# Issuing the matmuls that read low parts last, within scores, value products, output and down pieces and gate and up products

## The chip, the core and the metric

The program runs on one core of one Trainium2 chip. The metric is the device time of one execution in microseconds; of the kernel before there are three runs. A core has TensorE (matrix products into PSUM; PE in the rows, its weight loads PEld), VectorE (DVE), ScalarE (ACT), GpSimd (POOL), SyncE (SP) and DMA queues. Each engine works through its own instruction queue in order and waits at semaphores for the others.

## What is computed

```
h = layernorm(x) * (1 + ca) + sa                  # x: 2048 x 576; sa..gb from silu(c) @ w_mod
q = h @ wq                                        # 32 heads of 128; 16 key/value heads
p = softmax(q @ k.T / sqrt(128))                  # the last 512 keys of the cache, all rows
x = x + ga * ((p @ v) @ wo)
h = layernorm(x) * (1 + cb) + sb
x = x + gb * ((relu(h @ W_gate) * (h @ W_up)) @ W_down)   # 576 -> 4608 -> 576
```

All of it is in float32.

## The kernel before

Every float32 operand is split in two parts of TensorE's reduced format: a high part (a rounded copy, made by ScalarE) and a low part (the value minus the high part, made by GpSimd, for `qlo` by VectorE). A product a x b becomes three matmuls into one PSUM accumulation: high x high, high x low and low x high. So each group of three needs two low parts, and these are the last of the operands to be ready.

The attention part runs over 128 units (L1651): a unit is one head and one block of 512 rows. In unit u TensorE issues, in the order that is written out by hand in that loop (the schedule is manual):

- the scores of unit u, `s_half` (L488), two halves of two key tiles each: `k` is stationary, `qhi` and `qlo` stream, 512 columns; VectorE reduces each half to its maximum (L501),
- the query projection of unit u + 1 (`qps`, L424, 14 matmuls), from which ScalarE makes `qhi` and VectorE `qlo` (L480),
- in units below 4 and from 108 on the small product `qm` (L530) by which the maxima are spread; it waits for VectorE's L522. In units below 4 the maxima (`mr`) are subtracted by matmuls (L587),
- an output piece (`wo_piece` of an earlier pair of heads: a 128 x 576 block in two column halves, each in its own PSUM bank, six matmuls of 288 columns in each half),
- the value product of unit u - 1, `pv_half` (L626), two halves of six matmuls of 512 columns: `hi` and `lo` are the exponentials' parts,
- a second output piece, and then the next unit.

`o_mul` (L641, VectorE) divides the finished value product by the sums. The output pieces take `ohi` and `olo` of a pair of heads as stationary and `woga` (or `againo`, read back by a DMA) as streaming operand, high and low in `w[0]` and `w[1]`. A piece's PSUM tile has one buffer; for most pieces a ScalarE copy (L693) puts the running sum into it first (the seed), after another copy (L669) has taken the piece before out of it.

The MLP part (from about 1590 us) runs over pairs of hidden tiles: `prod` (L1007) makes gate and up with seven matmuls into one bank each; `wop` holds three tiles of high parts (the third with some low rows in it) and two of low parts. GpSimd writes the low rows of the third tile (L794) and then the two low tiles (L795). `md_piece` uses the same `down_piece` (L651) as the attention output.

Of the kernel before, what the change touches and what calls it, by code (L numbers as in the profile page):

```python
# [25 lines left out]
H2 = D // 2  # L26
# [8 lines left out]
def kernel(  # L35
# [13 lines left out]
    nc = tc.nc  # L49
# [399 lines left out]
    NU = HKV * NQB * 2  # L449
# [6 lines left out]
    wqs, ks, vs, wos = {}, {}, {}, {}  # L456
    qhi, qlo, pthi, ptlo, ohi, olo = {}, {}, {}, {}, {}, {}
    pt_src = {}

    def unit(u):  # L460
        return UNITS[u]
# [21 lines left out]
    st_, t5, pt, hi_, lo_, bc, rb, ks_, pvps, done, o, bps = ({} for _ in range(12))  # L483
# [4 lines left out]
    def s_half(u, h):  # L488
        g, qb, hd = unit(u)
        k = ks[g]  # L490
        t = psS.tile([P, 2, 512], F32, tag="s", name=f"s{u}_{h}")
        st_[u, h] = t
        for j in range(2):
            kt = 2 * h + j
            ps = t[:, j, :]
            nc.tensor.matmul(ps, k[:, kt, :], qhi[u], start=True, stop=False)  # L496
            nc.tensor.matmul(ps, k[:, 4 + kt, :], qhi[u], start=False, stop=False)  # L497
            nc.tensor.matmul(ps, k[:, kt, :], qlo[u], start=False, stop=True)  # L498
        if h == 0:
            t5[u] = sp.tile([P, 12, 16], F32, tag="t5", name=f"t5_{u}", bufs=1)  # L500
        nc.vector.tensor_reduce(t5[u][:, 2 * h:2 * h + 2, :].rearrange("p k b -> p (k b)"),  # L501
                                t.rearrange("p k (b j) -> p (k b) j", j=32),
                                axis=AX.X, op=ALU.max, apply_transpose=True)
# [122 lines left out]
    def pv_half(u, h):  # L626
        g, qb, hd = unit(u)
        if h == 0:
            pvps[u] = psM.tile([P, 512], F32, tag="mm", name=f"pv{u}")
        ps, v, a, b = pvps[u], vs[g], hi_[u, h], lo_[u, h]  # L630
        for j in range(2):
            kt = 2 * h + j
            nc.tensor.matmul(ps, v[:, kt, :], a[:, j, :], start=(kt == 0), stop=False)  # L633
            nc.tensor.matmul(ps, v[:, 4 + kt, :], a[:, j, :], start=False, stop=False)  # L634
            nc.tensor.matmul(ps, v[:, kt, :], b[:, j, :], start=False, stop=(kt == 3))  # L635
        if h:
            done[u] = pvps.pop(u)

    def o_mul(u):
        o[u] = rb.pop(u)  # L640
# [10 lines left out]
    def down_piece(his, los, ws, i, qt, nm, pool=None, seed=None):  # L651
        sl = slice(qt * P, (qt + 1) * P)
        pool = pool or (psW, "w")
        ps = pool[0].tile([P, 2, 512], F32, tag=pool[1], name=nm) if seed is None else seed
        for half in range(2):
            cs = slice(half * H2, (half + 1) * H2)
            n = 0
            for hi, lo, w in zip(his, los, ws):
                for a, b in ((hi, 0), (hi, 1), (lo, 0)):
                    nc.tensor.matmul(ps[:, half, :H2], a[:, sl], w[b][:, cs],  # L660
                                     start=(n == 0 and seed is None), stop=(n == 5),
                                     skip_group_check=seed is not None)
                    n += 1
        av = acc[i].rearrange("p (h n) -> p h n", h=2)

        def add():
            adds[i] += 1
            if seed is not None:
                nc.scalar.copy(av, ps[:, :, :H2])  # L669
                return  # L670
            nc.vector.tensor_tensor(av, ps[:, :, :H2], av, op=ALU.add)  # L671

        return add
# [21 lines left out]
    def piece(n):  # L695
        add = wo_piece(*pieces[n][1:], seed=seeds.get(n))

        def end():
            add()
            put_seed(n + 1)  # L700

        (pend_act if n in seeds else pend).append(end)
        return n in seeds
# [303 lines left out]
    def prod(m, s, n, xx):  # L1007

        hs, w = hop[m // NFP, OPS[s][1]], wop[n]
        ps = pair[m, s][:, xx, :]  # L1010
        ops = []
        for t in range(2):
            ops += [(w[:, xx, t, :], hs[t]), (w[:, xx, 3 + t, :], hs[t]), (w[:, xx, t, :], hs[3 + t])]
        ops.append((w[:, xx, 2, :], hs[2]))
        for i, (a, c) in enumerate(ops):
            nc.tensor.matmul(ps, a, c, start=s not in heir(m) and i == 0 and s not in seeds_of(m), stop=i == len(ops) - 1,  # L1016
                             skip_group_check=True)
# [268 lines left out]
    def step(name, t, fn, *args):  # L1286
        sched.append((t + PLAN.get(name, 0), len(sched), fn, args))

    HOOK = (0, 4, 6, 9)
    e = 10 * NU  # L1290
# [298 lines left out]
    t = 546  # L1589
# [32 lines left out]
    step("M1", e + 1, next, mlp)  # L1622
    step("T.pv0", e + 2, pv_half, NU - 1, 0)
    step("T.pv1", e + 2, pv_half, NU - 1, 1)
    step("T.sum", e + 2, sum_pre, NU - 1)
    step("M2", e + 3, next, mlp)
    step("T.mix", e + 4, last_unit)
# [7 lines left out]
    def run(u, k):  # L1635
        t = 10 * u + k
        while sched and sched[-1][0] <= t:
            fn, args = sched.pop()[2:]
            fn(*args)
# [11 lines left out]
    for u in range(NU):  # L1651
# [51 lines left out]
        run(u, 6)  # L1703
        if 0 < u < NU - 1:
            pv_half(u - 1, 1)
        if 10 * u + 6 in at:
            piece(at[10 * u + 6])
        run(u, 7)
        if u:
            o_mul(u - 1)  # L1710
# [63 lines left out]
```

## Time and profile before

| | us |
|---|---|
| runs, median of three (lowest to highest) | 2861.74 (2859.02 to 2862.04) |
| profiled execution: span from the first to the last instruction | 2855.8 |
| TensorE busy in the span | 2815.0 |
| VectorE busy | 2246.8 |
| GpSimd busy | 2123.8 |
| ScalarE busy | 1476.7 |

The span is 5.9 us shorter than the median of the runs; what lies around it is not in the rows. TensorE's granted clock was at the higher of its two levels nearly throughout (mean 0.998). A matmul's record ends by a model, later than the next matmul starts, so "busy" and "idle" of TensorE are read together with the starts.

### The profile page before, as it was taken

How to read it: one execution, taken by the hardware profiler on the slowest of the kernel's cores; microseconds unless marked ns; L12 is line 12 of the kernel's file. 1: busy time of each engine (PE TensorE's matmuls, PEld its weight loads, DVE VectorE, ACT ScalarE, POOL GpSimd, SP SyncE). 2: the span in 40 equal slices, each digit the busy share in tenths (PEclk: the TensorE clock that was granted, in tenths of full speed). 3: DMA queues.
4: the chain of work that ended last, by engine and by line, in shares of the span. 5: the costliest groups of instructions: out<-in, count | busy, mean ns of one | idle time of the engine just before them, and what ended most of it. 6: DMA issues, size and time to landing. Idle time of an engine off the chain costs nothing.

```text
span 2855.8 us, 41174 instructions
## 1 busy us (share of the span) xinstructions
PE 2815.0 (99%) x15006; PEld 2449.5 (86%) x15006; DVE 2246.8 (79%) x3384; ACT 1476.7 (52%) x2105; POOL 2123.8 (74%) x1564
## 2 busy tenths in 40 slices
PE   6999999999999999999999999999999999999999
PEld 5788888888888888888888888888888888888888
DVE  7899999999889998888889756676677466666666
ACT  5766666666766666666656444444444122222221
POOL 5688888888899989877778766788777356656653
PEclk9999999999999999999999999999999999999999
DMA  4012132222232213312243456666667844444442
GB/s 163 24 45 79 65 106 85 83 82 100 95 104 94 92 62 131 105 70 80 68 155 139 150 213 229 231 240 231 234 234 261 338 165 154 155 155 159 159 154 106
DMA packets 164506, 399.57 MB, mean 140 GB/s; under 512 B 15056, under 2 KB 62160, under 8 KB 164304
## 3 DMA queue, kind: packets, MB, share of 16 engines
q1 hardware_dynamic: 132912, 284.69, 29.9%
q10 hardware_dynamic: 31392, 112.26, 10.0%
q8 instruction: 118, 1.93, 0.3%
q14 instruction: 84, 0.69, 0.1%
HBM read 271.16 MB, written 154.57 MB: 149 GB/s over the span
## 4 chain that ended last, share of the span: by engine, by line
PE 83%; DVE 6%; POOL 5%; issue 2%; ACT 2%; DMA 2%; SPq 0%; ACTq 0%; DVEq 0%; POOLq 0%
PE gu L1016 26%; PE wo L660 12%; PE qps L424 11%; PE md L660 8%; PE st_P L1118 6%; PE s L498 3%; PE s L497 3%; PE s L496 3%; PE pv L635 3%; PE pv L634 3%; PE pv L633 3%; POOL lo L600 2%; DVE t L501 1%; DVE p L591 1%; POOL wop L795 1%
## 5 line engine op out<-in xcount | busy, mean ns | idle before, releaser
L600 POOL TENSOR_TENSOR lo<-p,hi 128x1024 fp32r<-128x1024 f32 x256 | 610.6, 2406 | 1.1 <-ACT hi L577 1.1
L609 POOL TENSOR_TENSOR ks<-ks,p 128x512 f32<-128x512 f32 x256 | 351.7, 1374 | 238.7 <-DVE ks L606 135.5
L501 DVE TRANSPOSE_TENSOR_REDUCE t<-s 128x32 f32<-128x1024 f32 x256 | 313.8, 1239 | 85.9 <-PE s L498 76.6
L1016 PE MATMUL gu<-hop_B,wop 128*128 128x512 f32 x1512 | 375.0, 391 | 0.2 <-POOL wop L795 0.2
L1016 PEld LDWEIGHTS gu<-hop_B,wop 128*128 128x128 f32 x1512 | 274.9, 188 | 51.1 <-POOL wop L795 0.9
L1016 PE MATMUL gu<-hop_T,wop 128*128 128x512 f32 x1260 | 316.1, 391 | 0.0
L424 PE MATMUL qps<-hTa,wA 128*128 128x512 f32 x1288 | 312.9, 394 | 3.1 <-DVE hTa L372 1.6
L660 PE MATMUL wo<-woga,ohi 128*128 128x288 f32 x1472 | 298.8, 295 | 2.0 <-POOL woga L183 1.4
L591 DVE TENSOR_TENSOR p<-s,mb 128x1024 f32<-128x1024 f32 x246 | 290.3, 1219 | 4.2
L424 PEld LDWEIGHTS qps<-hTa,wA 128*128 128x128 f32 x1288 | 244.5, 190 | 56.6 <-DVE hTa L372 3.2
L476 ACT ACTIVATE qhi<-qps 128x512 fp32r<-128x512 f32 x128 | 76.4, 597 | 366.9 <-PE qps L424 358.4
L660 PEld LDWEIGHTS wo<-woga,ohi 128*128 128x128 f32 x1472 | 245.9, 188 | 18.8 <-POOL woga L183 3.4
L1016 PEld LDWEIGHTS gu<-hop_T,wop 128*128 128x128 f32 x1260 | 227.8, 188 | 39.0
L577 ACT CAST hi<-p 128x1024 fp32r<-128x1024 f32 x256 | 259.5, 1042 | 1.5
L660 PE MATMUL md<-wogb,hhi 128*128 128x288 f32 x1272 | 256.9, 295 | 0.4 <-DVE acc L671 0.4
L593 ACT ACTIVATE p<-p 128x1024 f32<-128x1024 f32 x246 | 249.5, 1051 | 13.7 <-DVE p L591 13.4
L671 DVE TENSOR_TENSOR acc<-md,acc 128x576 f32<-128x576 f32 x159 | 119.9, 755 | 160.4 <-PE md L660 159.8
L660 PEld LDWEIGHTS md<-wogb,hhi 128*128 128x128 f32 x1272 | 210.9, 188 | 12.6 <-DVE acc L671 1.4
L1127 DVE TENSOR_TENSOR acc<-st_P,acc 128x576 f32<-128x576 f32 x160 | 121.1, 757 | 127.9 <-PE st_P L1118 127.9
L660 PE MATMUL wo<-woga,olo 128*128 128x288 f32 x736 | 217.8, 296 | 1.3 <-POOL olo L649 1.2
L660 PE MATMUL md<-wogb,hlo 128*128 128x288 f32 x636 | 187.5, 295 | 0.0
L649 POOL TENSOR_TENSOR olo<-rb,ohi 128x512 fp32r<-128x512 f32 x128 | 167.4, 1308 | 15.2 <-ACT ohi L645 15.0
(283 smaller groups left out, 7095.3 us busy)
## 6 DMA issues: line engine op xcount, KB each, us to landing
wop<-wk_P SPq DMA_DIRECT2D x133, 640.0 KB
wk_P<-wop ACTq DMA_DIRECT2D x119, 640.0 KB
wr<-wlay SPq DMA_DIRECT2D x68, 384.0 KB
rogb<-wd SPq DMA_DIRECT2D x68, 288.0 KB
againq<-akq SPq DMA_DIRECT2D x18, 640.0 KB
rwA<-wq SPq DMA_DIRECT2D x32, 320.0 KB
wlay<-wg SPq DMA_DIRECT2D x36, 256.0 KB
roga<-wo SPq DMA_DIRECT2D x32, 288.0 KB
```

The costliest lines, as they stand in the source:

```text
L424: return [lambda i=i, a=a, b=b: nc.tensor.matmul(ps, a, b, start=(i == 0), stop=(i == n - 1)) for i, (a, b) in enumerate(ops)]
L501: nc.vector.tensor_reduce(t5[u][:, 2 * h:2 * h + 2, :].rearrange("p k b -> p (k b)"), t.rearrange("p k (b j) -> p (k b) j", j=32), axis=AX ...
L577: nc.scalar.copy(hi_[u, h], pt[u, h])
L591: nc.vector.tensor_tensor(p, t, bc[u][:, None, :].to_broadcast([P, 2, 512]), op=ALU.subtract)
L593: nc.scalar.activation(p, p, AF.Exp, bias=0.0, scale=1.0)
L600: nc.gpsimd.tensor_sub(lo_[u, h], pt[u, h], hi_[u, h].bitcast(F32))
L609: nc.gpsimd.tensor_tensor(ks_[u], ks_[u], p[:, j, :], op=ALU.add)
L649: nc.gpsimd.tensor_sub(olo[u], o.pop(u), ohi[u].bitcast(F32))
L660: nc.tensor.matmul(ps[:, half, :H2], a[:, sl], w[b][:, cs], start=(n == 0 and seed is None), stop=(n == 5), skip_group_check=seed is not None)
L1016: nc.tensor.matmul(ps, a, c, start=s not in heir(m) and i == 0 and s not in seeds_of(m), stop=i == len(ops) - 1, skip_group_check=True)
L1118: nc.tensor.matmul(ps[:, j, :H2], x[:, sl], w[:, y, :], start=n == 0 and not second, stop=n == 2, skip_group_check=True)
L1127: nc.vector.tensor_tensor(t, ps[:, :, :H2], t, op=ALU.add)
```

## The change

In four places the matmuls that read a low part come after those that read only high parts, as far as the group goes; the operands and the sums are the same.

- `s_half`: the two key tiles' high products first, then the two that read `qlo`.
- `pv_half` leaves the `lo` products out; a new `pv_lows` issues all four. It stands directly behind the second `pv_half` in odd units; in even units the second output piece stands in between.
- `down_piece` (output and down pieces): in each column half four matmuls (both high x high, the first low x high, the first high x low), then in each half the other two.
- `prod`: the products with `wop`'s low tiles come last, with the third tile ahead of them.

```
-            ps = t[:, j, :]
-            nc.tensor.matmul(ps, k[:, kt, :], qhi[u], start=True, stop=False)
-            nc.tensor.matmul(ps, k[:, 4 + kt, :], qhi[u], start=False, stop=False)
-            nc.tensor.matmul(ps, k[:, kt, :], qlo[u], start=False, stop=True)
+            nc.tensor.matmul(t[:, j, :], k[:, kt, :], qhi[u], start=True, stop=False)
+            nc.tensor.matmul(t[:, j, :], k[:, 4 + kt, :], qhi[u], start=False, stop=False)
+        for j in range(2):
+            nc.tensor.matmul(t[:, j, :], k[:, 2 * h + j, :], qlo[u], start=False, stop=True)
...
-            nc.tensor.matmul(ps, v[:, kt, :], b[:, j, :], start=False, stop=(kt == 3))
-        if h:
-            done[u] = pvps.pop(u)
+    def pv_lows(u):
+        g, qb, hd = unit(u)
+        ps, v = pvps.pop(u), vs[g]
+        for kt in range(4):
+            nc.tensor.matmul(ps, v[:, kt, :], lo_[u, kt // 2][:, kt % 2, :], start=False, stop=kt == 3)
+        done[u] = ps
...
-            for hi, lo, w in zip(his, los, ws):
-                for a, b in ((hi, 0), (hi, 1), (lo, 0)):
+        ops = [(his[0], ws[0][0]), (his[1], ws[1][0]), (los[0], ws[0][0]), (his[0], ws[0][1]),
+               (his[1], ws[1][1]), (los[1], ws[1][0])]
+        for part in ((0, 1, 2, 3), (4, 5)):
+            for half in range(2):
...
-            ops += [(w[:, xx, t, :], hs[t]), (w[:, xx, 3 + t, :], hs[t]), (w[:, xx, t, :], hs[3 + t])]
-        ops.append((w[:, xx, 2, :], hs[2]))
+            ops += [(w[:, xx, t, :], hs[t]), (w[:, xx, t, :], hs[3 + t])]
+        ops += [(w[:, xx, 2, :], hs[2]), (w[:, xx, 3, :], hs[0]), (w[:, xx, 4, :], hs[1])]
...
             pv_half(u - 1, 1)
+            if u % 2:
+                pv_lows(u - 1)
         if 10 * u + 6 in at:
             piece(at[10 * u + 6])
+        if 0 < u < NU - 1 and u % 2 == 0:
+            pv_lows(u - 1)
```

TensorE, first half of the scores of unit 45, before and then after (names carry the unit; `kv5_0` is the key tile set):

```order
L496 MATMUL s45_0_6300<-qhi45_6222,kv5_0_5419 128x512
L497 MATMUL s45_0_6300<-qhi45_6222,kv5_0_5419 128x512
L498 MATMUL s45_0_6300<-qlo45_6260,kv5_0_5419 128x512
L496 MATMUL s45_0_6300<-qhi45_6222,kv5_0_5419 128x512
L497 MATMUL s45_0_6300<-qhi45_6222,kv5_0_5419 128x512
L498 MATMUL s45_0_6300<-qlo45_6260,kv5_0_5419 128x512
```

```order
L495 MATMUL s45_0_6300<-qhi45_6222,kv5_0_5419 128x512
L496 MATMUL s45_0_6300<-qhi45_6222,kv5_0_5419 128x512
L495 MATMUL s45_0_6300<-qhi45_6222,kv5_0_5419 128x512
L496 MATMUL s45_0_6300<-qhi45_6222,kv5_0_5419 128x512
L498 MATMUL s45_0_6300<-qlo45_6258,kv5_0_5419 128x512 x2
```

The two matmuls that read `qlo45` stood third and sixth; now they are fifth and sixth. Both key tiles' sums are open at once, each in its bank.

TensorE, even unit 66: the second half of the value product of unit 65 and the start of the piece behind it, before; then the end of that piece and what follows it, after:

```order
L633 MATMUL pv65_9015<-hi65_1_8933,kv8_1_8685 128x512
L634 MATMUL pv65_9015<-hi65_1_8933,kv8_1_8685 128x512
L635 MATMUL pv65_9015<-lo65_1_8940,kv8_1_8685 128x512
L633 MATMUL pv65_9015<-hi65_1_8933,kv8_1_8685 128x512
L634 MATMUL pv65_9015<-hi65_1_8933,kv8_1_8685 128x512
L635 MATMUL pv65_9015<-lo65_1_8940,kv8_1_8685 128x512
L660 MATMUL wo63_2_9023<-woga_14_7792,ohi62_8689 128x288 x2
L660 MATMUL wo63_2_9023<-woga_14_7792,olo62_8691 128x288
L660 MATMUL wo63_2_9023<-woga_15_8113,ohi63_8876 128x288 x2
```

```order
L666 MATMUL wo63_2_9021<-woga_14_7792,ohi62_8689 128x288 x2
L666 MATMUL wo63_2_9021<-woga_15_8113,ohi63_8876 128x288
L666 MATMUL wo63_2_9021<-woga_14_7792,olo62_8691 128x288
L666 MATMUL wo63_2_9021<-woga_14_7792,ohi62_8689 128x288
L666 MATMUL wo63_2_9021<-woga_15_8113,ohi63_8876 128x288
L666 MATMUL wo63_2_9021<-woga_15_8113,olo63_8878 128x288
L666 MATMUL wo63_2_9021<-woga_15_8113,ohi63_8876 128x288
L666 MATMUL wo63_2_9021<-woga_15_8113,olo63_8878 128x288
L640 MATMUL pv65_9015<-lo65_0_8938,kv8_1_8685 128x512 x2
L640 MATMUL pv65_9015<-lo65_1_8940,kv8_1_8685 128x512 x2
```

The four reads of `lo65` are behind the piece now, directly ahead of the scores of unit 67. In the piece the reads of `olo63` (the pair's second head) are the last of each half.

TensorE, the gate product `gu45` of one hidden tile, before and after (`hop0_B11_0` to `_2` are high parts, `_3` and `_4` low; an x2 reads a high and then a low weight tile):

```order
L1016 MATMUL gu45_19733<-hop0_B11_0_16355,wop63_19657 128x512 x2
L1016 MATMUL gu45_19733<-hop0_B11_3_16358,wop63_19657 128x512
L1016 MATMUL gu45_19733<-hop0_B11_1_16356,wop63_19657 128x512 x2
L1016 MATMUL gu45_19733<-hop0_B11_4_16359,wop63_19657 128x512
L1016 MATMUL gu45_19733<-hop0_B11_2_16357,wop63_19657 128x512
```

```order
L1021 MATMUL gu45_19733<-hop0_B11_0_16355,wop63_19657 128x512
L1021 MATMUL gu45_19733<-hop0_B11_3_16358,wop63_19657 128x512
L1021 MATMUL gu45_19733<-hop0_B11_1_16356,wop63_19657 128x512
L1021 MATMUL gu45_19733<-hop0_B11_4_16359,wop63_19657 128x512
L1021 MATMUL gu45_19733<-hop0_B11_2_16357,wop63_19657 128x512
L1021 MATMUL gu45_19733<-hop0_B11_0_16355,wop63_19657 128x512
L1021 MATMUL gu45_19733<-hop0_B11_1_16356,wop63_19657 128x512
```

The products with the two low weight tiles were second and fifth (the second of each x2) and are now the last two. On VectorE, ScalarE and GpSimd the instructions stand in the same order before and after.

## Rows read from the trace of the kernel before

**Rows 1.** The page: busy time of each engine, share, instructions
```profile
PE 2815.0 (99%) x15006; PEld 2449.5 (86%) x15006; DVE 2246.8 (79%) x3384; ACT 1476.7 (52%) x2105; POOL 2123.8 (74%) x1564
```

**Rows 2.** Table by stage, 600 to 1000 us: length, busy time by engine, clock, DMA
```profile
600.00:1000.00 400.00, 396.95 (x2070) 343.51 (x2069) 362.80 (x616) 275.12 (x382) 357.50 (x229) 1.00 0.29 94
```

**Rows 3.** TensorE's waits: who waited for whom, us in total, times, longest us
```profile
PE wo L660 <- POOL woga L183: 1.4, 3, 0.7
PE wo L660 <- POOL olo L649: 1.2, 5, 0.5
PE pv L635 <- POOL lo L600: 1.1, 2, 0.6
PE s L498 <- DVE qlo L480: 0.9, 2, 0.7
PE gu L1016 <- POOL wop L795: 0.6, 3, 0.2
PE wo L660 <- DMA againo<-ako: 0.3, 1, 0.3
```

**Rows 4.** The weight loads' waits, same columns
```profile
PEld pv L635 <- POOL lo L600: 3.9, 9, 1.0
PEld wo L660 <- POOL woga L183: 3.4, 8, 0.9
PEld s L498 <- DVE qlo L480: 3.4, 5, 1.1
PEld wo L660 <- POOL olo L649: 2.7, 6, 0.7
PEld gu L1016 <- POOL wop L795: 2.6, 7, 0.6
```

**Rows 5.** Timeline of TensorE around two waits: start us, length us, instruction, [idle before]
```profile
479.01 0.30 PE L660 MATMUL wo<-woga,ohi 128*128 128x288 f32 x1
479.67 0.40 PE L660 MATMUL wo<-woga,ohi 128*128 128x288 f32 x1 [0.36 <-POOL woga L183]
481.08 0.40 PE L497 MATMUL s<-qhi,kv 128*128 128x512 f32 x1
481.62 0.50 PE L498 MATMUL s<-qlo,kv 128*128 128x512 f32 x1
481.95 0.40 PE L496 MATMUL s<-qhi,kv 128*128 128x512 f32 x1
```

**Rows 6.** Timeline of unit 80 (even): seed copy and the second piece
```profile
1017.82 0.64 ACT L669 COPY acc<-wo 128x576 f32<-128x576 f32 x1 [1.04 <-PE wo L660]
1018.49 0.64 ACT L693 COPY wo<-acc 128x576 f32<-128x576 f32 x1
1020.31 0.42 PE L660 MATMUL wo<-woga,ohi 128*128 128x288 f32 x2
1020.97 0.29 PE L660 MATMUL wo<-woga,olo 128*128 128x288 f32 x1
1021.10 0.43 PE L660 MATMUL wo<-woga,ohi 128*128 128x288 f32 x2
```

**Rows 7.** Timeline of units 124 and 125: `o_mul`, scores, L522, `qm`
```profile
1554.91 0.68 DVE L641 TENSOR_TENSOR rb<-pv,rb 128x512 f32<-128x512 f32 x1
1555.62 0.39 PE L496 MATMUL s<-qhi,againk 128*128 128x512 f32 x1
1560.66 0.70 DVE L522 TRANSPOSE_TENSOR_REDUCE t<-ks 128x16 f32<-128x512 f32 x1
1561.55 0.34 PE L530 MATMUL qm<-t,quad 128*128 128x80 f32 x2
```

**Rows 8.** Timeline of unit 1: `mr`, the fifth value matmul, the matmuls that need `mr`
```profile
57.62 0.62 ACT L569 CAST mr<-mb 128x512 fp32r<-128x512 f32 x1 [7.67 <-DVE mb L566]
57.98 0.39 PE L634 MATMUL pv<-hi,kv 128*128 128x512 f32 x1
58.44 1.09 PE L587 MATMUL s<-mr,minus 128*128 128x512 f32 x4
```

More of the change, by code (lines that the diff above doesn't have):

```diff
@@ L629, in pv_half @@
             pvps[u] = psM.tile([P, 512], F32, tag="mm", name=f"pv{u}")
-        ps, v, a, b = pvps[u], vs[g], hi_[u, h], lo_[u, h]
+        ps, v, a = pvps[u], vs[g], hi_[u, h]
         for j in range(2):
@@ L654, in down_piece @@
         ps = pool[0].tile([P, 2, 512], F32, tag=pool[1], name=nm) if seed is None else seed
-        for half in range(2):
-            cs = slice(half * H2, (half + 1) * H2)
-            n = 0
-            for hi, lo, w in zip(his, los, ws):
-                for a, b in ((hi, 0), (hi, 1), (lo, 0)):
-                    nc.tensor.matmul(ps[:, half, :H2], a[:, sl], w[b][:, cs],
+        ops = [(his[0], ws[0][0]), (his[1], ws[1][0]), (los[0], ws[0][0]), (his[0], ws[0][1]),
+               (his[1], ws[1][1]), (los[1], ws[1][0])]
+        for part in ((0, 1, 2, 3), (4, 5)):
+            for half in range(2):
+                cs = slice(half * H2, (half + 1) * H2)
+                for n in part:
+                    a, w = ops[n]
+                    nc.tensor.matmul(ps[:, half, :H2], a[:, sl], w[:, cs],
                                      start=(n == 0 and seed is None), stop=(n == 5),
                                      skip_group_check=seed is not None)
-                    n += 1
         av = acc[i].rearrange("p (h n) -> p h n", h=2)
@@ L1624 @@
     step("T.pv1", e + 2, pv_half, NU - 1, 1)
+    step("T.pv2", e + 2, pv_lows, NU - 1)
     step("T.sum", e + 2, sum_pre, NU - 1)
```

## Prediction

> **What bounds the kernel now.** I read four views. The page's busy line comes first: TensorE is busy 2815.0 of 2855.8 us [rows 1], so no other engine can give back more than the gaps in its stream. The table by stage says how far the others are behind it: between 600 and 1000 us TensorE works 396.95 of 400 us, VectorE 362.80 and GpSimd 357.50 [rows 2]. TensorE is the bound, and the two that make the operands run close enough to be late now and then. The third view, TensorE's waits [rows 3], lists where: on `lo` (GpSimd) in the value product, on `olo` and the low half of `woga` (GpSimd) in the output pieces, on `qlo` (VectorE) in the scores, on the low rows of `wop` (GpSimd) in gate and up. Together 1.1 + 1.2 + 1.4 + 0.9 + 0.6 = 5.2 us in 15 waits. The weight loads' own list has the same five names, 3.9 + 2.7 + 3.4 + 3.4 + 2.6 = 16.0 us in 35 waits [rows 4]. Those two sums are the bounds of what this change can touch.
>
> The fourth view shows what one wait costs. Output matmuls start 0.13 us apart; at 479.01 the next started only at 479.67, 0.53 late, though the row calls 0.36 of it idle [rows 5]. A score matmul's record is 0.39 to 0.40 long while the next one starts 0.23 later [rows 5, 8]: the record's last 0.16 us hides as much of every wait. And the start after a wait is late once more: 481.62 to 481.95 is 0.33 instead of 0.23 [rows 5]. So a wait with idle time costs its idle time + 0.16 + 0.10.
>
> The Trainium skill's page "TensorE: Matmul & The Clock Gate" (section "Step-by-step: what each phase is for") says that weight loads are pulled ahead of matmuls in flight, so the next weights load while this matmul runs. By that rule the second delay would not exist and 15 × 0.10 = 1.5 us would fall out of the sum; the start at 481.95 speaks against it here, since the load behind a waiting one came late as well.
>
> **What the change removes.** No instruction comes or goes; the same matmuls stand in another order, and VectorE, ScalarE and GpSimd keep theirs. Sum of the waits: 5.2 + 15 × 0.16 + 15 × 0.10 = 9.1 us. In the 20 other waits only the load was late: each costs between nothing and 0.26 us, I take half, 2.6. That is 11.7 us, between 5.2 and 16.0.
>
> How much of each goes depends on how far its reader moves back.
> - Value product: in an even unit the second half's low read goes from ninth place to behind a whole output piece (two matmuls of 0.23 and twelve of 0.13 more): 2 us, against waits of at most 0.6 + 0.16 [rows 3]. Gone. In odd units it moves two matmuls, 0.45 us.
> - Scores: the first read of `qlo` goes from third to fifth, 0.45 us. The longest wait cost 0.7 + 0.16 = 0.86; 0.41 stays, and its 0.10.
> - Output pieces: the low half of the second weight goes from fifth to ninth, the second `olo` from sixth to tenth, 4 × 0.13 = 0.53 us. Of the longest waits 0.86 - 0.53 = 0.33 and 0.66 - 0.53 = 0.13 stay, with 0.10 each.
> - Gate and up: the low rows go from second to sixth, 0.9 us, against at most 0.2 + 0.16. Gone.
>
> What stays: 0.51 + 0.43 + 0.23 = 1.2 us. Gain: 11.7 - 1.2 = 10.5 us.
>
> **What it costs.** Four things are moved nearer to what they wait for.
> - In even units the value product now ends behind the piece, right ahead of the next scores, and `o_mul` (L641) on VectorE waits for it. In front of the scores that began at 1555.62 it started at 1554.91 [rows 7]; the last low matmul would start 0.23 before the scores and be done 0.39 after its start, at 1555.78: 0.87 later. Queued behind it are the L886 combinations, the two score reductions and L522. Where VectorE sat idle before the next reduction that is free. From 1520 to 1590 it did not: L522 ended at 1561.36 and the `qm` matmul that needs it ran at 1561.55 [rows 7], 0.19 of slack. So `qm` waits 0.87 - 0.19 = 0.68 us, three times (behind units 122, 124 and 126, where the same work stands on VectorE): 2.0 us. Bounds: 0 and 3 × 0.87 = 2.6.
> - In units 1 to 3 the first half of the value product covers the making of `mr`: six matmuls up to 58.44, `mr` done at 58.24 [rows 8]. With four, TensorE is there at 57.98 and waits 0.26 + 0.10; three times, 1.1 us (nothing, if a later wait of that stage shrinks by it).
> - In a piece the second pair's high halves are read two matmuls earlier; the one wait on `againo` [rows 3] grows by 0.26 us.
> - In even units the second piece starts four matmuls, 0.91 us, earlier. Its PSUM tile is seeded by a ScalarE copy that ended at 1019.13, the piece began at 1020.31 [rows 6]: of 1.18 us 0.27 stay. I take nothing.
>
> The 119 more waits in gate and up (the third weight tile now asks for itself) cost nothing where they are met when reached; the seven late loads on `wop` [rows 4] are what the trace has of the other kind.
>
> Costs 2.0 + 1.1 + 0.3 = 3.4. Net 10.5 - 3.4 = 7.1 us. The profiled span would become 2848.7; the median of the runs stands 5.9 above the span and I keep that: **2861.7 - 7.1 = 2854.6 us**. A measurement of this kernel can tell about 0.2%, 5.7 us, from no change, so this lies just beyond it, at 2856.0.
>
> **The rivals.**
> 1. *The waits come back.* A TensorE that is earlier meets the next late operand: VectorE had 37 and GpSimd 42 us of slack in 400 [rows 2]. For it: a wait also gives the late engine time to catch up. Against it: the reads that follow move back by 0.45 us or more too. If half the gain returns, 5.2 - 3.4 = 1.8 us: 2859.9.
> 2. *The waits cost what the loads show.* 16.0 - 1.2 - 3.4 = 11.4 us: 2850.3. For it: every late load delays what is behind it. Against: a load is early by up to one matmul, and part of its wait is free.
> 3. *Slower: the seed copy.* The margin left in even units is 0.27 us [rows 6], 63 units, of which 233 in 256 pieces have such a copy, so about 57. Each 0.1 us by which the copy comes later than that costs 57 × 0.1 = 5.7 us; it eats the whole gain from 0.27 + 7.1 / 57 = 0.40 us on. At 0.5 it is 57 × 0.23 = 13 us: 2867.7. For it: the copy stands on ScalarE between exponentials of 1 us. Against: ScalarE had been idle 1.04 us when the piece ended [rows 6], so nothing stands in front.
> 4. *The order itself costs.* Pieces and score halves now change their PSUM bank three times instead of once: two more in each of 416 pieces and 256 halves, 1344. At 1020.97 to 1021.10 such a change takes the usual 0.13 [rows 6]; the row is good to 5 ns, so up to 1344 × 0.005 = 6.7 us either way. On the bad side: 2861.3.
>
> That the build undoes the change is excluded by the order of instructions.
>
> **How the numbers follow.** The forecast 0.55, rival 1 0.20, rival 2 0.14, rival 3 0.05, rival 4 0.06. Faster by over 0.2% (below 2856.0): rival 2 whole and most of the forecast, 0.14 + 0.48 = 0.62. Within: the rest of the forecast, rivals 1 and 4, 0.07 + 0.20 + 0.06 = 0.33. Slower: 0.05. The range goes from a little under rival 2, since its costs may be nothing, to between rivals 1 and 4: 2848.5 to 2861.0, which leaves out rival 3 and the tails.
>
> **What would show it.** Right: the five names nearly vanish from TensorE's waits, one each on `qlo` and `woga` left under 0.5 us; the span is 6 to 8 us shorter; new entries are `qm` on VectorE's L522 near 1530, 1555 and 1580 of about 0.7 and `s` on `mr` three times. Rival 1: the names stay with fewer microseconds each. Rival 3: the seed copy L693 (L698 there) heads the releasers of output pieces. Rival 4: no waits, but matmuls of unchanged number in more busy time. The forecast is wrong if the five names go and the span does not follow.

## The result and the profile after

| | before | after |
|---|---|---|
| runs on one chip, median of eight each (lowest to highest), us | 2860.22 (2857.31 to 2862.04) | 2866.68 (2862.70 to 2867.57) |
| profiled execution: span, us | 2855.8 | 2860.6 |

The ratio is 1.0022, with a 95% interval of 1.0013 to 1.0031: the change made the kernel slower by about 6 us where 7 less were forecast. The predicted range ended at 2861.0. One execution of e2 below, 3086.97 us at a granted clock of 0.851, is in no median and no ratio here.

The page of the changed kernel, busy time and the chain that ended last:

```profile
PE 2817.1 (98%) x15006; PEld 2451.6 (86%) x15006; DVE 2249.3 (79%) x3384; ACT 1477.6 (52%) x2105; POOL 2123.9 (74%) x1564
...
PE 90%; DVE 5%; DMA 1%; POOL 1%; ACT 1%; issue 1%; SPq 0%; DVEq 0%; POOLq 0%; ACTq 0%
```

The chain stays on TensorE for 90% of the span. Its 15006 matmuls are busy 2.1 us longer than before [rows 1], and the span grew by 4.8; so some of the loss lies within busy time and some in new waits. TensorE's waits in the changed kernel (us in total, times, longest):

```profile
PE qm L530 <- DVE t L522: 5.7, 6, 1.3
PE s L587 <- ACT mr L569: 3.2, 3, 2.1
...
PE md L666 <- DVE acc L676: 2.4, 1, 2.4
...
PE s L498 <- DVE qlo L480: 0.8, 2, 0.6
PE wo L666 <- POOL woga L183: 0.7, 2, 0.3
PE gu L1021 <- DMA wop<-wk_P: 0.6, 1, 0.6
...
PE wo L666 <- POOL olo L653: 0.4, 1, 0.4
PE wo L666 <- DMA againo<-ako: 0.4, 1, 0.4
```

Beside [rows 3], what the change aimed at did happen: `lo` is gone from the list, `woga` and `olo` fell from 2.6 us in eight waits to 1.1 in three. The stage that was busiest with such waits shows it too: between 600 and 1000 us TensorE is busy 398.82 us, where [rows 2] had 396.95.

```profile
600.00:1000.00 400.00, 398.82 (x2081) 345.62 (x2080) 366.57 (x617) 276.41 (x383) 360.26 (x231) 1.00 0.29 94
```

New at the head of the list is `qm` behind VectorE, 5.7 us, and a down piece (`md`) with one wait of 2.4.

Where the 5 us came from is best read from landmarks: the start of the first score matmul of a unit, of the first gate and up product, and of the last matmul. The table has the difference to the same landmark in the trace of before, split into four stretches (us; minus is earlier). It lists all kernels of the experiments below; each row is one profiled execution.

| kernel | up to unit 12 | units 12 to 116 | unit 116 to the MLP | MLP | all |
|---|---|---|---|---|---|
| changed | +0.9 | -4.6 | **+7.0** | +1.8 | +5.1 |
| changed, again (e11) | +0.7 | -4.6 | +6.8 | +3.2 | +6.0 |
| no piece in between (e1) | -0.8 | -4.7 | -0.1 | -0.6 | -6.2 |
| piece in between to unit 107 (e4) | +2.8 | -4.6 | -0.1 | +0.4 | -1.5 |
| low products in mid piece (e5) | +1.3 | -3.6 | +0.9 | -0.6 | -2.1 |
| changed, piece as before (e2) | +0.2 | -0.9 | +7.5 | +6.5 | +13.4 |
| before, only the piece changed (e3) | -1.3 | -2.8 | 0.0 | +6.9 | +2.7 |
| e1, bank after bank (e6) | +3.0 | -0.8 | -0.1 | +1.4 | +3.6 |
| e1, four-six-two (e7) | +2.3 | -8.4 | -0.4 | -0.7 | -7.1 |
| e1, early lows inside (e8) | +1.2 | -4.5 | -0.1 | -1.1 | -4.4 |
| e1, alternating (e9) | +0.4 | -7.3 | -0.3 | +4.5 | -2.7 |
| changed, four-six-two (e10) | +1.1 | -7.7 | +6.8 | +1.4 | +1.6 |
| before, four-six-two (e12) | 0.0 | -6.2 | -0.4 | +2.0 | -4.5 |

The second and third columns repeat: the changed kernel's two profiles agree within 0.3 us there. The first and the last don't; what lies in them is told in the last section.

### The profile page after: what moved, and what is told of

The parts are those of the page before. It is cut to its first block, busy times and chain, and to the rows that moved or that the text cites. A ratio compares the mean times of both kernels' runs of the same rounds, so it can differ in the third digit from the quotient of the medians.

```text
span 2860.6 us, 41113 instructions
## 1 busy us (share of the span) xinstructions
PE 2817.1 (98%) x15006; PEld 2451.6 (86%) x15006; DVE 2249.3 (79%) x3384; ACT 1477.6 (52%) x2105; POOL 2123.9 (74%) x1564
## 4 chain that ended last, share of the span: by engine, by line
PE 90%; DVE 5%; DMA 1%; POOL 1%; ACT 1%; issue 1%; SPq 0%; DVEq 0%; POOLq 0%; ACTq 0%
PE gu L1021 28%; PE wo L666 13%; PE qps L424 12%; PE md L666 9%; PE st_P L1123 6%; PE pv L633 4%; PE s L495 4%; PE pv L634 4%; PE pv L640 4%; PE s L498 4%; PE s L496 4%; DVE t L501 1%; POOL lo L600 0%; DVE p L591 0%; DVE roga L223 0%
## 5 line engine op out<-in xcount | busy, mean ns | idle before, releaser
L609 POOL TENSOR_TENSOR ks<-ks,p 128x512 f32<-128x512 f32 x256 | 351.2, 1372 | 239.0 <-DVE ks L606 129.1
L676 DVE TENSOR_TENSOR acc<-md,acc 128x576 f32<-128x576 f32 x159 | 119.9, 755 | 164.5 <-PE md L666 164.0
L666 PE MATMUL wo<-woga,olo 128*128 128x288 f32 x736 | 211.2, 295 | 0.6 <-POOL olo L653 0.4
```

What stands on the lines that cost most here:

```text
L609: nc.gpsimd.tensor_tensor(ks_[u], ks_[u], p[:, j, :], op=ALU.add)
L666: nc.tensor.matmul(ps[:, half, :H2], a[:, sl], w[:, cs], start=(n == 0 and seed is None), stop=(n == 5), skip_group_check=seed is not None)
```

## The loss at the end of the attention part

Theory A: the output piece that now stands ahead of the low value products makes `o_mul` late, and by it VectorE's row of work up to `qm`. The prediction had this step, at 2.0 us. Here is unit 125 in the changed kernel: the first score matmul, `o_mul` (L645), the two combinations (L891), GpSimd's L609, L522 and `qm` (start, length, idle before):

```profile
1554.76 0.40 PE L495 MATMUL s<-qhi,againk 128*128 128x512 f32 x1
1554.96 0.69 DVE L645 TENSOR_TENSOR rb<-pv,rb 128x512 f32<-128x512 f32 x1 [0.83 <-PE pv L640]
1555.08 3.00 POOL L609 TENSOR_TENSOR ks<-ks,p 128x512 f32<-128x512 f32 x2 [1.75 <-ACT p L593]
1555.57 1.37 DVE L891 TENSOR_TENSOR lfb<-lfb,lfb 128x512 f32<-128x512 f32 x1
1556.85 1.77 DVE L891 TENSOR_TENSOR h<-h,h 128x512 f32<-128x512 f32 x1
...
1561.39 0.70 DVE L522 TRANSPOSE_TENSOR_REDUCE t<-ks 128x16 f32<-128x512 f32 x1
...
1562.15 0.45 PE L530 MATMUL qm<-t,quad 128*128 128x80 f32 x2 [1.32 <-DVE t L522]
```

and the two rows of the kernel before that answer to L609 and the first L891 (there L886):

```profile
1555.51 0.68 DVE L886 TENSOR_TENSOR lfb<-lfb,lfb 128x512 f32<-128x512 f32 x1
...
1555.95 3.10 POOL L609 TENSOR_TENSOR ks<-ks,p 128x512 f32<-128x512 f32 x2 [1.74 <-ACT p L593]
```

`o_mul` started 0.71 us ahead of the scores [rows 7] and now starts 0.20 behind them: 0.91 later, where 0.87 was predicted. But the combination behind it takes 1.37 us instead of 0.68. Before, it started 0.44 ahead of GpSimd's L609; now L609 is already under way. So the delay is 0.91 + 0.69 = 1.60, less the slack of 0.19 it is 1.41; `qm` runs 7.39 us after the first score matmul instead of 5.93 [rows 7], 1.46 later. Of the slack 0.13 could be used: L522 ends at 1562.09 here and `qm` starts 0.06 behind it.

**e1, no piece in between.**

```
             pv_half(u - 1, 1)
-            if u % 2:
-                pv_lows(u - 1)
+            pv_lows(u - 1)
...
-        if 0 < u < NU - 1 and u % 2 == 0:
-            pv_lows(u - 1)
```

> The changed kernel, but the low value products stand directly behind the second half of the value product in every unit; no output piece in between. Theory A (the piece in between makes o_mul late on VectorE, and with it L522 and qm; the units from 118 to the start of the MLP lost 7.0 us in the trace): that stage gives 6 to 7 us back, the waits of qm and of the scores on mr around 1590 us go, and the time is about 2860. In even units the low products move only 0.45 us back instead of 2, so at most 0.5 us of waits on lo come back. Theory B (the whole loss is the dearer start of 512-column matmuls behind a piece in its new order, 12 to 16 ns at some 400 places): the piece in between does not add such places, so the time stays at about 2866.

Measured: 2852.35 against 2858.61 of before on that chip, ratio 0.9981 (0.9972 to 0.9990). The stage lost nothing (-0.1), `qm` stands as it stood before, 5.93 us after the scores, and its waits are these:

```profile
PE qm L530 <- DVE t L522: 1.1, 2, 0.6
```

Theory A holds, theory B as the only cause falls. The gain was larger than the 6 to 7 us expected: by the landmarks e1 is 11.3 us ahead of the changed kernel, 7.1 of them in this stage, 2.4 in the MLP, where no down piece (below) waited, and 1.7 in the first units, which vary from one execution to the next.

**e4, the piece in between only below unit 108.**

```
-            if u % 2:
+            if u % 2 or u >= 108:
                 pv_lows(u - 1)
...
-        if 0 < u < NU - 1 and u % 2 == 0:
+        if 0 < u < 108 and u % 2 == 0:
             pv_lows(u - 1)
```

> The changed kernel, with the output piece ahead of the low value products in even units below 108 only; from 108 on, where qm runs again, the low products stand directly behind the value product. Theory A (the place of the loss is the qm stage): the same gain as without any piece in between, about 2860, and below unit 108 the same times at each unit as in the changed kernel. Rival (the piece in between costs in all units, by o_mul running beside other work on VectorE and GpSimd): less than half of the gain, 2863.5 or more, while the version without any piece in between has all of it.

Measured: 2852.93, ratio 0.9980 (0.9972 to 0.9989), as without any piece in between. The place is the units from 108 on. Between units 12 and 116 the two versions gained the same (4.6 and 4.7), so the piece in between brought nothing where it cost nothing: two matmuls of distance were as good as fourteen. In e1 0.7 us of late starts on `lo` stayed in these units, and others were shorter by as much.

**e5, the low products in the middle of the piece.** Here the push is made smaller, to tell whether the wait grows in step with it or by the stretched combination; `midway` holds the low products of an even unit.

```
+    midway = []
...
         for part in ((0, 1, 2, 3), (4, 5)):
+            if part == (4, 5) and midway:
+                midway.pop()()
             for half in range(2):
...
                 pv_lows(u - 1)
+            else:
+                midway.append(lambda u=u: pv_lows(u - 1))
...
-        if 0 < u < NU - 1 and u % 2 == 0:
-            pv_lows(u - 1)
+        if midway:
+            midway.pop()()
```

> The changed kernel, but in even units the low value products stand in the middle of the output piece (behind its first eight matmuls), not behind it. The value product then ends four matmuls of 0.13 earlier against the next scores: o_mul is pushed by 0.87 - 0.53 = 0.34 us instead of 0.87. Linear theory (each qm loses the push minus the 0.19 of slack): 0.15 us in units 119, 123, 125 and 127 in place of 1.11, 1.50, 1.48 and 1.21, the stage from unit 118 to the MLP gives 6 of its 7 us back. Collision theory (the two-operand VectorE instruction behind o_mul is stretched as soon as it runs beside GpSimd's next instruction): part of the waits stay at 0.5 us and more, although the push is only 0.34.

One run: 2855.24 against 2859.39 of before. The stage lost 0.9 us instead of 7.0, and unit 125 reads so (the combination stands on L895 there):

```profile
1554.12 0.68 DVE L895 TENSOR_TENSOR lfb<-lfb,lfb 128x512 f32<-128x512 f32 x1
...
1554.17 3.50 POOL L609 TENSOR_TENSOR ks<-ks,p 128x512 f32<-128x512 f32 x2 [1.75 <-ACT p L593]
...
1560.05 0.45 PE L530 MATMUL qm<-t,quad 128*128 128x80 f32 x2
```

VectorE's combination started 0.05 us ahead of GpSimd's L609, took its 0.68, and GpSimd's pair of instructions took 3.50 instead of 3.10. `o_mul` was pushed by 0.39 (0.34 expected) and `qm` was 0.28 late, near the 0.15 of the linear theory; unit 123 reads the same, and at units 119 and 127 `qm` was on time within 0.06. So in the changed kernel's unit 125 the linear part is 0.91 - 0.19 = 0.72 and the stretched instruction adds 0.69; in these rows the second appears only when the push carries VectorE past GpSimd's start.

The Trainium skill has a rule for this pair, on the page "SBUF — State Buffer", in the section "Who interferes with whom": VectorE and GpSimd share one pair of SBUF ports, held exclusively by one of them at a time. The rows agree in who gives way: where GpSimd had started first VectorE's combination took 0.69 us longer, and in e5, where VectorE had started 0.05 ahead, GpSimd's pair took 0.40 longer. Both prices are this case's.

## The order within a piece

Theory B: after a piece in its new order the 512-column matmuls start in a dearer rhythm (they stand further apart, from start to start). Twelve of them behind a piece took 2743 ns from start to start (median of 115) in the kernel before and 2758 in the changed one, the piece itself 1584 and 1582. In single steps the starts stood 224, 231, 236, 228, 233, 231 and then 227 ns apart; now 233, 236, 224, 231, 236, 228, 232, 231 and then 227.

**e2, the changed kernel with the old order of the piece; e3, the kernel before with the new order of the piece.** The edits are the `down_piece` part of the diff, taken back in the one and made alone in the other.

> The changed kernel with the order of the output and down pieces of the kernel before (one column half after the other, high high, high low, low high for each head). Theory B: the 512-column matmuls behind a piece start in the old rhythm again, some 400 places of 12 to 16 ns, 5 us less; the waits on olo and woga come back, which took 2.6 us of idle time and by the prediction's sum 4.1 us in all: net about -1 us, 2865.5. Rival (the order within the piece costs nothing): only the waits come back, +4 us, 2870.5.

> The kernel before, with only the new order within the output and down pieces. Theory B: +5 us by the dearer starts behind a piece, -4 us by the waits on olo and woga that go: 2861, no change that can be told. Rival (the order within the piece costs nothing): 2860.2 - 4 = 2856.

Measured: e2 2868.39 (four runs, 2865.37 to 2872.70), ratio 1.0038 (1.0024 to 1.0052); e3 2859.28, ratio 1.0005 (0.9996 to 1.0013), by its ratio near the 2861 of theory B. The rhythm followed the order of the piece, 2743 in e2 and 2758 in e3, with one exception: in e2 the pieces that stand in between, eight matmuls behind another piece, left 2758 behind them (median of 61) in spite of their old order, and took 1589 themselves. Such a piece, the first low product behind it and the thirteenth matmul behind it:

```profile
1018.88 0.43 PE L664 MATMUL wo<-woga,ohi 128*128 128x288 f32 x2
...
1020.47 1.09 PE L640 MATMUL pv<-lo,kv 128*128 128x512 f32 x4
...
1023.23 0.39 PE L495 MATMUL s<-qhi,kv 128*128 128x512 f32 x1
```

So what stands ahead of a piece counts as well. e2 was no faster than the changed kernel (1.0038 against 1.0022, the intervals overlap), and its profile ended 8.3 us later. Of these, 4.7 lie in the MLP, where two down pieces started 2.57 us late each (in the changed kernel one, 2.52), and 3.7 between units 12 and 116. The waits tell of the latter, the first two lines; the other two are from e3:

```profile
PE wo L664 <- POOL woga L183: 3.2, 6, 1.2
PE wo L664 <- POOL olo L653: 1.7, 3, 0.6
```

```profile
PE s L498 <- DVE qlo L480: 2.0, 3, 1.0
PE pv L635 <- POOL lo L600: 1.0, 2, 0.5
```

With scores and value products in the new order and pieces in the old one, `woga` and `olo` cost 4.9 us instead of the 2.6 of before [rows 3]; with pieces in the new order alone, `qlo` cost 2.0 instead of 0.9. A wait taken away in one group could come back in the next. At 479.67 the kernel before waited for `woga`, and at 481.62 the start was 0.31 late on `qlo` [rows 5]; in e3 the first wait was gone and the second had become 0.83 late, the whole 0.52 handed on:

```profile
479.07 0.40 PE L497 MATMUL s<-qhi,kv 128*128 128x512 f32 x1
480.12 0.50 PE L498 MATMUL s<-qlo,kv 128*128 128x512 f32 x1 [0.66 <-DVE qlo L480]
```

Between units 12 and 116 e2 gained 0.9 us and e3 2.8, the changed kernel with both 4.6.

**e6, bank after bank; e7, four-six-two; e9, alternating.** All three are e1 with the same new order of operands, in which the second weight's low half and the second low part come last; only the way through the two column halves (two PSUM banks) differs. The loops around the matmul of a piece, in the changed kernel (and e1) and in e6:

```
-        for part in ((0, 1, 2, 3), (4, 5)):
-            for half in range(2):
...
-                for n in part:
...
+        for half in range(2):
...
+            for n, (a, w) in enumerate(ops):
```

The new loops in e7, and then in e9:

```
+        for half, part in ((0, (0, 1, 2, 3)), (1, (0, 1, 2, 3, 4, 5)), (0, (4, 5))):
...
+            for n in part:
```

```
+        for n, (a, w) in enumerate(ops):
             for half in range(2):
```

> The version without the piece in between, with the new order of operands in a piece, but one column half (one PSUM bank) whole before the other. If the two more changes of bank make the 512-column matmuls behind a piece start in the dearer rhythm (233 236 224 231 236 228 232 231 ns instead of 224 231 236 228 233 231), the twelve behind a piece take 2743 ns again. If the order of operands does it, they stay at 2758. The low half of the second weight and the second olo are read fifth and sixth again, so the waits on woga and olo come back, some 4 us. Net: about -1 us of the rhythm and +4 against the version without the piece in between.

> The version without the piece in between, with each piece as four matmuls of the first half, all six of the second, and the last two of the first: two changes of bank instead of three, and the late operands are still read ninth and later. If the rhythm behind a piece depends on how the piece ends, it goes back to 2743 ns: 220 places in the attention part and 125 in the MLP, 5 us less than that version, and 2847 in all. If not, the time is that version's, 2852.

> The version without the piece in between, with the two column halves of a piece (two PSUM banks) alternating from matmul to matmul, in the new order of operands: eleven changes of bank in a piece. If each change of bank costs (the prediction's rival 4, 5 ns each), a piece and the twelve 512-column matmuls behind it take 8 x 5 = 40 ns more than the 1582 + 2758 ns of three changes, 7 us in the attention part and 7 in the MLP more than that version: 2866. If it is not the number of changes but their sequence (four, six, two with two changes took 1590 + 2723, less than 1584 + 2743 with one), no such growth: 2847 to 2852.

Measured: e6, one run, 2860.85 beside 2859.39 of before; e7 2846.79, ratio 0.9954 (0.9942 to 0.9966), the lowest of all medians; e9 2850.82, ratio 0.9971 (0.9958 to 0.9983).

| way through the banks | changes of bank | piece, ns | twelve behind it, ns | sum |
|---|---|---|---|---|
| six, six (before, e6) | 1 | 1584 | 2743 | 4327 |
| four, six, two (e7) | 2 | 1590 | 2723 | 4313 |
| four, four, two, two (changed, e1) | 3 | 1582 | 2758 | 4340 |
| alternating (e9) | 11 | 1584 | 2743 | 4327 |

The rows show it to 10 ns. Each block below has the start of a piece, the first matmul of the value product behind it and the start of the next piece; before, e1 and e7 in this order:

```profile
1004.16 0.42 PE L660 MATMUL wo<-woga,ohi 128*128 128x288 f32 x2
...
1005.74 0.39 PE L633 MATMUL pv<-hi,kv 128*128 128x512 f32 x1
...
1008.48 0.42 PE L660 MATMUL wo<-woga,ohi 128*128 128x288 f32 x2
```

```profile
1011.25 0.42 PE L666 MATMUL wo<-woga,ohi 128*128 128x288 f32 x2
...
1012.84 0.40 PE L633 MATMUL pv<-hi,kv 128*128 128x512 f32 x1
...
1015.60 0.42 PE L666 MATMUL wo<-woga,ohi 128*128 128x288 f32 x2
```

```profile
1000.52 0.42 PE L665 MATMUL wo<-woga,ohi 128*128 128x288 f32 x2
...
1002.11 0.39 PE L633 MATMUL pv<-hi,kv 128*128 128x512 f32 x1
...
1004.83 0.42 PE L665 MATMUL wo<-woga,ohi 128*128 128x288 f32 x2
```

That is 2.74, 2.76 and 2.72 us for the same twelve matmuls. e6 has the new order of operands and the old rhythm, so the way through the banks sets it, with what stands ahead (e2), and not the operands. But it is not a price for each change: eleven changes cost as much as one, two less, three more. The new order of the score halves, which also goes to and fro between banks, cost nothing: the twelve score matmuls behind a piece took 2743 ns in e6 too. Why the sequence matters was not settled.

By their ratios e7 is 0.0027 of 2859, 7.7 us, faster than e1; summed over the starts of the two profiles, the rhythm gave 5.0 us between units 12 and 116 and 3.9 in the MLP. Some of it was lost again, in e7's profile to a transfer for which TensorE waits:

```profile
PE gu L1020 <- DMA wop<-wk_P: 3.0, 1, 3.0
```

**e10, the changed kernel with four-six-two; e12, the kernel before with four-six-two.** The edit is e7's; in e12 it brings the new order of operands into the pieces as well.

> The changed kernel whole, with the output piece in between, but each piece as four, six and two matmuls by column half. The rhythm behind the pieces gives back 27 ns at some 345 places, less where the two low products and the scores follow each other: 7 to 9 us; the stage from unit 118 to the MLP keeps its loss of 7.0. Both causes add up: 2865 - 8 = 2857, a little below the kernel before. Rival (what the rhythm gives is lost again in later waits): 2862 or more.

> The kernel before with one edit: each piece as four, six and two matmuls by column half, with the late operands last. Scores, value products and gate and up as before. The rhythm takes 14 ns less for a piece and what follows it (4313 instead of 4327) at some 345 places, 4.8 us; the waits on woga and olo go as they did with the changed kernel's order of the piece, 2.8 us between units 12 and 116: 2858.5 - 7.6 = 2851. If the waits that go come back on qlo and lo in the same unit (the rival by which a wait is only handed on), 2854. The version that also has the other three edits took 2846.8, so those would be worth 4 to 7 us on top.

Measured: e10 2857.43, ratio 0.9993 (0.9984 to 1.0002); e12 2852.95, ratio 0.9986 (0.9977 to 0.9995). e10 keeps the loss of the last units (+6.8) and gains 3.1 us more than the changed kernel between units 12 and 116: two causes that add. e12 gained 6.2 between units 12 and 116, where 5.7 was expected as the sum of rhythm (2.9) and waits (2.8), and lost 3.9 again at one down piece's wait in the MLP and what stood around it; the granted clock was 0.50, the 1.2 GHz level, from 1976.1 to 1979.5 us, during that wait and behind it. The other edits are then worth e7 against e12, 0.0032 of 2859 or 9 us by the ratios; e12's profile had that wait and e7's had not.

## The first units, and the changed kernel a second time

**e8, the low products of units 0 to 3 inside the value product, as before.** This is e1 with one more edit:

```
             nc.tensor.matmul(ps, v[:, 4 + kt, :], a[:, j, :], start=False, stop=False)
+            if u < 4:
+                nc.tensor.matmul(ps, v[:, kt, :], lo_[u, h][:, j, :], start=False, stop=kt == 3)
...
-        for kt in range(4):
+        for kt in range(4 if u >= 4 else 0):
```

> The version without the piece in between, with the low products of units 0 to 3 back inside the value product, as in the kernel before. The prediction's step (the four matmuls left no longer cover the making of mr, 0.36 us each in units 1 to 3): the starts of the matmuls on mr that came 0.31 to 0.32 late in units 1 and 2 are on time, and 0.6 to 1.1 us comes back between units 0 and 4. Rival (a later wait of that stage absorbs it): the waits go, and unit 8 starts at the same time after unit 0 as without it.

One run: 2853.17 beside 2859.39. The waits of the predicted step are there in the changed kernel, in unit 1:

```profile
57.64 1.20 PE L587 MATMUL s<-mr,minus 128*128 128x512 f32 x4 [0.15 <-ACT mr L569]
```

The start is 0.31 late, in units 1 and 2, where 0.36 was predicted. In e8 both are gone, and the wait on VectorE's L372 in unit 3 is longer by as much (e1 above, e8 below):

```profile
77.72 0.95 PE L329 MATMUL lta<-ident,xna 128*128 128x128 f32 x7 [1.14 <-DVE hTa L372]
```

```profile
78.78 0.96 PE L329 MATMUL lta<-ident,xna 128*128 128x128 f32 x7 [1.69 <-DVE hTa L372]
```

So the rival holds for the most part: the step cost 0.6 us in two units and gave most of them back in the next. From unit 0 to unit 8 e8 took 112.05 us, and e5 and e10, whose stretches at the lower clock there are as long as e8's, 112.21 and 112.19: 0.1 to 0.2 us stayed. (e1 took 109.91; its stretches at the lower clock are shorter.)

**e11, the changed kernel once more, unaltered.**

> The changed kernel, unaltered, a second profile. Three stages outside the theories differed from the kernel before in its one trace: the first five units (+2.1 us at unit 4), the down piece that waited 2.4 us for VectorE behind an instruction of 6.0 us near 1980 us (+2.6), and 0.75 us on a DMA of wop near 2237. If they belong to the change, they come again at the same size; if they are a matter of how the engines happen to stand to each other in one execution, the size or the place differs. The stage from unit 118 to the MLP loses 7.0 us again in either case.

One run: 2863.29 beside 2858.47. The last units lost 6.8 us again, with `qm` late by 1.11, 1.51, 1.51 and 1.21 at units 119, 123, 125 and 127 (1.11, 1.50, 1.48 and 1.21 in the first trace). The down piece waited again at the same place, 2.55 us. The first units did not repeat: from unit 0 to unit 7 the first profile lost 1.2 us and this one gained 1.3, and the wait on `wop` near 2238 us was 1.46 instead of 0.75. No size of these two can be put down to the change; over the fourteen traces the idle time on that transfer ranges from none (e8) to 3.4 us (e9).

## Why the prediction was wrong

**The gain** was about right. This is summed over the starts of both traces, one by one: a start that stands over 20 ns further behind the one before than usual (227 ns for 512 columns, 132 for 288) is late by the difference, and what is left is the rhythm. Between units 12 and 116 the late starts fell from 14.2 us to 7.2, and the rhythm took 2.4 more; hence the 4.6 of the landmarks. In the MLP, outside the down piece's wait and the `wop` transfer, 3.2 us of late starts went against 1.8 of rhythm. Together 10.2, predicted 10.5. The shares were less right. Of `qlo`, `woga` and `olo` starts 3.1 us late stayed, where 1.2 with `againo` aside were to stay, since waits were handed on (rival 1 in small): at 591 us `qlo` was still 0.72 late, at 768 and 863 `woga` 0.50 and 0.47. That the sum still came out is in part luck: in the trace of before the late starts at readers of the five names and right behind them add up to some 13 us, not 11.7, so the late loads cost more than the half that I took.

**The forecast failed on two terms of its costs**: `qm`, 2.0 us with an upper bound of 2.6, whose stage lost 7.0; and the order itself, which the sum had at nothing and which took 4.2 (rival 4, below). Had either of the two alone been as forecast, the account below would have come out 0.1 or 0.9 us longer than before, and not 7.1 shorter.

At `qm` three things were mis-sized. The events were four, not three: unit 119 has the same wait, behind another combination, which took 1.78 us where it took 0.69 before:

```profile
1480.70 1.78 DVE L913 TENSOR_TENSOR hy_B<-h,hy_B 32x512 fp32r<-32x512 f32 x1
...
1484.12 0.69 DVE L908 TENSOR_TENSOR hy_B<-h,hy_B 32x512 fp32r<-32x512 f32 x1
```

Each cost 1.1 to 1.5 us, not 0.68, since the push was worked out with VectorE's durations of before, and the push itself changes which of VectorE and GpSimd starts first. And in unit 127 the wait was not the last: `mr` came 1.03 us late behind it, and after these two waits TensorE's clock fell to its lower level.

```profile
1588.00 0.45 PE L530 MATMUL qm<-t,quad 128*128 128x80 f32 x2 [1.05 <-DVE t L522]
1588.25 1.59 PE L619 MATMUL pv<-lo,againv 128*128 128x512 f32 x4
1590.70 2.05 PE L587 MATMUL s<-mr,minus 128*128 128x512 f32 x4 [0.86 <-ACT mr L569]
```

The four matmuls on `mr` take 2.05 us; in unit 1 above they take 1.20. The table by stage puts the granted clock from 1590.8 to 1592.6 at 0.50, the 1.2 GHz level, and it stays there to 1594.1:

```profile
1590.80:1592.60 1.80, 1.80 (x5) 1.41 (x6) 0.59 (x1) 1.51 (x3) 1.27 (x1) 0.50 0.38 150
1590.80:1594.10 3.30, 3.30 (x11) 2.91 (x12) 1.65 (x3) 2.98 (x5) 1.27 (x1) 0.50 0.21 82
```

All four traces that keep the piece in between to the end (changed, e11, e2, e10) have the lower clock at this place, and none of the other ten. Of the 7.0 us, 5.3 are the four waits on `qm`, 1.0 the wait on `mr`, about 1.2 the lower clock and the rest rhythm; a wait on `lo` in unit 127, 1.31 late before and 0.32 now, gave 1.0 back.

**Rival 4**, that the order itself costs, had 0.06 and a bound of 6.7 us. It cost 2.4 + 1.8 = 4.2, at the pieces alone. The row that I weighed it by was the one change of bank in a piece of before, 0.13 us as any other start [rows 6]; the cost lay not at the change but in the starts behind the piece. The trace of before had a sign of it that the prediction passed over: there too the twelve starts behind a piece take 2743 ns and not twelve times 226.7, 23 more. What another order would make of them it could not show, since every piece there had the same order.

**The other steps.** The cover of `mr`: 0.31 in two units, absorbed, net nothing (predicted 1.1, with nothing as a bound). `againo`: its start is 0.53 late instead of 0.45, +0.08 (predicted 0.26). The seed copy (rival 3): no output piece waits for one, as forecast. The 119 more waits on `wop`: the list has `wop` only behind its DMA, once; that wait comes with the old order of `prod` as well (2.1 us late in e3). The even units' piece in between, counted as a gain of distance, brought nothing that two matmuls didn't (e4).

**What no step had**: the down piece's wait of 2.4 us in the MLP, told below. With it the account closes: gain 10.2; `qm`'s stage 7.0, rhythm 4.2, down piece 2.6, first units 0.9, the `wop` transfer 0.6; net 5.1 us longer, the landmarks' difference. The median of the runs grew by 6.5; the profiled execution, 2863.28, was among the shorter of the eight.

Of what the prediction said would refute it, "the five names go and the span does not follow" is what came in the main (`qlo`, `woga` and `olo` kept 1.9 us of idle time), and its own lines on `qm` and on rival 4 were the places to look.

## What to carry to other kernels

Moving late reads back within their group paid about what was worked out, and two matmuls of distance were as good as fourteen; moving the end of a group back delays whoever reads the whole group, so follow that engine's row of work with the durations it will have at its new times, not with the old ones. Waits that follow each other closely should not simply be added: the 0.52 us taken from the wait on `woga` (made by GpSimd) stood whole on `qlo` (made by VectorE) 2 us later. And where the order of short matmuls is free, time some orders: four-six-two against four-four-two-two was 27 ns for each piece and what follows it.

## What the runs showed of the hardware

**A margin of 0.1 us decided a stretch of 5 us.** The down piece that waited in the changed kernel waited for L676, which stood behind a VectorE sum of two SBUF operands (L828) that took 6.04 us:

```profile
1980.36 0.81 POOL L799 TENSOR_TENSOR wop<-wr,wop 32x256 fp32r<-32x256 f32 x1 [1.83 <-ACT wop L798]
...
1980.49 6.04 DVE L828 TENSOR_TENSOR wr<-wr,wr 128x768 f32<-128x768 f32 x1
...
1987.26 0.54 PE L666 MATMUL md<-wogb,hhi 128*128 128x288 f32 x2 [2.36 <-DVE acc L676]
```

The same place in e1:

```profile
1971.59 0.95 DVE L828 TENSOR_TENSOR wr<-wr,wr 128x768 f32<-128x768 f32 x1
...
1971.63 1.50 POOL L799 TENSOR_TENSOR wop<-wr,wop 32x256 fp32r<-32x256 f32 x1 [2.02 <-ACT wop L798]
```

In all fourteen traces there are 238 such sums. At the start of nine of them an instruction of GpSimd had been running for 0.03 to 0.61 us, and these nine took 6.04 to 6.09 us. At the start of the other 229 none was running, and they took 0.94 to 0.95. Which of the two it is depends on how the engines stand to each other after all that went before; the changed kernel had it in both its profiles and e2 twice in its one, e3, e6, e9, e10 and e12 once, and the kernel before, e1, e4, e5, e7 and e8 not at all. Whether the change brings it is not shown. The section "SBUF: two separate sides" of the same page of the Trainium skill says that the engine that starts first holds the shared port pair for its whole instruction. That agrees; but the 6.04 us of VectorE's sum here span five GpSimd instructions in a row (0.81, 1.28, 1.42, 1.27 and 0.71 us), not one. Whether another placement of L828 would avoid it was not tried.

**TensorE's starts depend on what stood ahead of them.** Pieces in different order leave the 512-column starts behind them 230 and then 227 ns apart (e7), or irregular between 224 and 236 for six to eight starts (before, changed), with 3 to 38 ns more in all than twelve times 226.7, the mean step in the long rows of query projections. In e2 the same piece left 2743 behind it after twelve or more matmuls of 512 columns and 2758 after eight, so the dependence reaches past the piece's own twelve matmuls.

**The first units hold stretches at the lower clock** (0.50, the 1.2 GHz level) whose length differs between executions of the same kernel. The one in unit 3, behind the wait for `hTa` (L372), held 8 matmuls in the trace of before (80.5 to 83.5 us), 14 in the changed kernel's first (85.5 to 92.3) and 9 in its second (88.1 to 91.5).
